# Attention with sinks and a window, then a gated feed-forward layer, on one core: batch 0 in runs of six column tiles, with the order of its requests and of the next batches' loads changed

## The chip, the cores and the metric

The kernel runs on one core of a Trainium2 chip. The metric is device time in microseconds, the median of several executions. Five engines work side by side, each through its own list of instructions in order: TensorE (PE: matrix products, with weight loads beside them), VectorE (DVE), ScalarE (ACT), GpSimd (POOL) and SyncE (SP, here only a queue that issues transfers). POOL also issues transfers, those that turn f32 into bf16 on the way.

## The reference

Inputs: q, k, v of 4 batches, 8 heads, 768 positions, 64 wide, in f32; the weights of the second layer, 512 x 1536 twice and 1536 x 512 once.

```python
scores = scale * np.matmul(q, k.transpose(0, 1, 3, 2))
is_sink = pos[None, :] < int(n_sink)              # n_sink = 4
rel = pos[:, None] - pos[None, :]
in_window = (rel >= 0) & (rel < int(window))      # window = 128
scores = np.where(is_sink | in_window, scores, -1000000000.0)
scores = scores - np.max(scores, axis=-1, keepdims=True)
a = np.exp(scores)
a = a / (np.sum(a, axis=-1, keepdims=True) + 1e-09)
attn_out = np.matmul(a, v)
...
x = attn_out.transpose(0, 2, 1, 3).reshape(B * S, H * D)      # 3072 x 512
gate = np.maximum(x @ w_gate, 0.0)
out = (gate * (x @ w_val)) @ w_out                            # 3072 x 512
```

## The kernel before

The work falls into 16 units: unit i is a pair of heads, number i % 4, of batch i // 4. A unit passes through these steps.

- Its k and q are loaded (`load_half` in two halves for batch 0, L110; `load_rows` for the others, L159) into one of three pairs of buffers, `kf` and `qf`, and turned to bf16 on POOL (`cast_half`, `cast_rows`) into one of two pairs, `kn` and `qn`.
- They are turned so that the 64 values of a head lie on partitions, into one of four `KQ` tiles: on PE for batches 0 and 1 (`T_half`, H in the plan, and `T`), and through DRAM with a transposing transfer for batches 2 and 3 (`to_dram` writes `kqd`, "td" in the plan; `turn` reads it back). POOL copies the keys of the odd tiles and the sinks (`odd_tiles`, L185).
- `Sg` (S in the plan, with unit and segment) makes a segment of scores on PE, ACT takes exp from PSUM into `ee` (L298), and DVE multiplies by the mask (L300).
- `W` makes the products with v on PE (L325) and divides on DVE (L330, L331) into `xn`. v comes through `load_v` and a cast (`cast_v`, L134).
- `X` turns `xn` on PE (L342) and ACT copies it to `xT` (L345). For batches 2 and 3 this goes through DRAM too (`x_to_dram`, `x_turn`).

`xT` of a batch, 512 x 768, is the input of the second layer. `chunk(b, g, m)` makes column tile m (128 of the 1536) of half g of the positions: four products with `wg` (L360), a Relu on ACT (L363, `gs`), four with `wv` (L365), and a product of both on DVE into `hT` (L367). Its two PSUM banks come from three, in turn. Half 0 of batch 0 has 372 positions and needs only the first three tiles of attention (part 0 of W and X), half 1 has 396. `ffn2` then multiplies `hT` by `wo` (L392).

Everything is in an order written out by hand. First comes a head: the loads and part 0 of batch 0's attention. Then 96 slots follow, each one chunk. In each slot the list `prep` is issued first (casts, loads, requests), then the chunk, then the list `plan` (H, T, S, W, X of a unit), then three `ffn2` products from slot 24 on. Batch 0's column tiles go in two runs, so that the first weights serve both halves before the later ones are needed:

```python
for b, runs in enumerate((((0, 8), (8, FM)),) + ((((0, FM),),) * (B - 1))):
    slots += [(b, g, m) for m0, m1 in runs for g in range(2) for m in range(m0, m1)]
```

So slots 0 to 7 are half 0 of tiles 0 to 7, slots 8 to 15 half 1 of the same, 16 to 23 tiles 8 to 11. The weights come in pieces, `load_w(m0, m1)`, issued by POOL between its casts: tiles 0-1, 2-3 and 4-5 in the head, 6-7 in slot 1 behind the first cast of later v tiles, 8-11 in slot 9, `wo` in slot 14.

Every engine and queue keeps to its list. A transfer on SP waits, in its place, for the buffer that it fills and for the eighth transfer before it. `gate(u)` (L138) is a memset of two elements of `kf` on DVE; the load of that buffer must wait for it, and so can't be issued before DVE has reached that place of its list. Before the change the loads of units 4 to 6 have such a gate in slot 6, and halves 4 and 5 one in the head (L423).

Of the kernel before, what the change touches and what calls it, by code (L numbers as in the profile page):

```python
# [21 lines left out]
def kernel(  # L22
# [12 lines left out]
    nc = tc.nc  # L35
# [80 lines left out]
    def cast_half(c, copies=(nc.gpsimd.tensor_copy, nc.gpsimd.tensor_copy)):  # L116
        for src, dst, copy in ((kf, kn, copies[0]), (qf, qn, copies[1])):
            copy(half(dst, c).rearrange("p (n h d) -> p h n d", n=3, h=2),
                                  half(src, c).rearrange("p (h n d) -> p h n d", n=3, h=2))
# [4 lines left out]
    def load_v(b, j, r0=0, r1=128):  # L124
        r1 = min(r1, S - VROW[j])

        parts = [(0, 4, 0), (4, 16, VROW[j] + 4), (16, 128, VROW[j] + 16)] if j in (1, 3, 5) else [(0, 128, VROW[j])]
        for a0, a1, s0 in parts:
            a1 = min(a1, r1)
            if r0 <= a0 < a1:  # L130
                nc.sync.dma_start(out=vf[a0:a1, j, :, :], in_=v[b, :, s0:s0 + a1 - a0, :].rearrange("h s d -> s h d"))
# [4 lines left out]
    def gate(u):  # L136

        nc.vector.memset(kf[u.i % NQ][0:1, 0:2], 0.0)  # L138
# [209 lines left out]

    gvn = [0]

    def chunk(b, g, m):
        assert all((b, p, g) in ready for p in range(NP)), (b, g)
        x, h = xT[b % 2], hT[b % 2]
        cut = CUT if b else CUT0
        c = slice(0, cut) if g == 0 else slice(cut, S)
        n = c.stop - c.start
        gp, vp = G[gvn[0] % 3], G[(gvn[0] + 1) % 3]
        gvn[0] += 2
        for ko in range(KO):
            nc.tensor.matmul(out=gp[:, 0:n], lhsT=wg[:, ko, m * 128:(m + 1) * 128], rhs=x[:, ko, c],  # L360
                             start=ko == 0, stop=ko == KO - 1)
        gs = gspool.tile([128, S - CUT0], F32, name="gs")
        nc.scalar.activation(gs[:, 0:n], gp[:, 0:n], Act.Relu, bias=0.0, scale=1.0)  # L363
        for ko in range(KO):
            nc.tensor.matmul(out=vp[:, 0:n], lhsT=wv[:, ko, m * 128:(m + 1) * 128], rhs=x[:, ko, c],  # L365
                             start=ko == 0, stop=ko == KO - 1)
        nc.vector.tensor_tensor(h[:, m, c], gs[:, 0:n], vp[:, 0:n], op=Alu.mult)  # L367

    OP = [[G[3][:]], [G[3][:], PP[0][:, 0, :], PP[1][:, 0, :]]]
# [29 lines left out]
    with tc.manual_schedule():  # L399
# [25 lines left out]
        for j in range(3):  # L425
            cast_v(0, j, copy=dve if j == 2 else nc.gpsimd.tensor_copy)
        load_w(2, 4)
        for c in range(4, 8):
            load_half(c)
            if c < 6:  # L430
                cast_half(c)
        for j in range(3, 7):
            load_v(0, j)
        load_w(4, 6)
        Sg(U[2], 0, PP[1])
        Sg(U[2], 3, PP[0])
        W(U[0], 0, g[2])
# [5 lines left out]
        X(U[1], 0, g[1])  # L443
        W(U[3], 0, PP[0][:, 0, :])
        X(U[2], 0, g[2])
        X(U[3], 0, g[3])
        setup2(1)
        setup2(2)


        slots = []

        for b, runs in enumerate((((0, 8), (8, FM)),) + ((((0, FM),),) * (B - 1))):
            slots += [(b, g, m) for m0, m1 in runs for g in range(2) for m in range(m0, m1)]
        plan = [[] for _ in slots]
        at = {}
# [3 lines left out]
            at[st] = s  # L460
            plan[s].append(st)

        for s, w in {0: "H0", 1: "S04 H1", 2: "S02 H2 S14", 3: "S12 H3", 4: "S24 S22", 5: "S34 S32", 6: "W01 W11",
                     7: "X01 W21 X11 W31 X21 X31"}.items():
            for y in w.split():
                put(s, y, 0)
        for s, w in {8: "T0", 9: "T1", 10: "S00 S01", 11: "T2", 12: "S02 S10", 13: "T3 S11", 14: "S12 S20", 15: "S21",
                     16: "S22 S30", 17: "S31 S32", 19: "W0", 20: "W1 X0", 21: "W2 X1", 22: "W3 X2", 23: "X3 F3"}.items():
            for y in w.split():
                if y[0] == "F":  # L470
                    plan[s].append(("F", int(y[1:]), 0))
                else:
                    put(s, y, 1)
        for b, sl in ((2, {28: "S00 S01", 30: "S02 S10", 32: "S11 S12", 34: "S20 S21", 35: "W0", 36: "S22 S30",
# [3 lines left out]
            for s, w in sl.items():  # L478
                for y in w.split():
                    put(s, y, b)  # L480
        prep = [[] for _ in slots]
        prep[1] += [("half", 6), ("half", 7), ("setup3",), ("v", 0, 3), ("w", 6, 8), ("v", 0, 4), ("v", 0, 5), ("v", 0, 6)]
        prep[6] += [("load", 4), ("load", 5), ("load", 6)]
        prep[8] += [("kq", 4), ("load", 7), ("lv", 1)]
        prep[9] += [("kq", 5), ("w", 8, 12)]
        prep[10] += [("kq", 6)]
        prep[11] += [("kq", 7)]
        prep[14] += [("v", 1, 0), ("v", 1, 1), ("v", 1, 2), ("v", 1, 3), ("wo",), ("v", 1, 4), ("v", 1, 5), ("v", 1, 6)]
        for i, ts in ((8, (18, 21, 22, 25)), (9, (19, 22, 23, 26)), (10, (21, 24, 25, 28)), (11, (23, 25, 27, 30)),
                      (12, (28, 31, 33, 36)), (13, (30, 33, 35, 38)), (14, (32, 35, 37, 42)), (15, (34, 37, 39, 43))):  # L490
            for t, what in zip(ts, ("rows", "castrows", "td", "turn")):
                prep[t].append((what, i))
            assert at["S", i - NP, 2] < ts[3] < at["S", i, 0] - 1, i
            prep[at["S", i, 0] - 1].append(("sinks", i))
            prep[at["W", i, 0] + 1].append(("xd", i))
            prep[at["W", i, 0] + 3].append(("xturn", i))

        for b, s0, s1 in ((2, 24, 28), (3, 44, 47)):
            for j in range(7):
                prep[s0 + j].append(("lv", b, j))  # L500
                prep[s1 + j].append(("v", b, j))

        f2 = deque()
        for s, (b, g, m) in enumerate(slots):
            for x in prep[s]:
                if x[0] == "kq":
                    cast_rows(U[x[1]])
                elif x[0] == "load":
                    if x[1] < 7:
                        gate(U[x[1]])  # L510
                    load_rows(U[x[1]])
                elif x[0] == "half":
                    cast_half(x[1])
                elif x[0] == "w":
                    load_w(*x[1:])
                elif x[0] == "wo":
                    for c in range(3):
                        load_wo(c)
                elif x[0] == "rows":
                    load_rows(U[x[1]])  # L520
                elif x[0] == "castrows":
                    cast_rows(U[x[1]])
                elif x[0] == "td":
                    to_dram(U[x[1]])
                elif x[0] == "setup3":
                    setup3()
                elif x[0] == "xd":
                    x_to_dram(U[x[1]])
                elif x[0] == "xturn":
                    x_turn(U[x[1]])  # L530
                elif x[0] == "turn":
                    turn(U[x[1]])
                elif x[0] == "sinks":
                    odd_tiles(U[x[1]], nc.gpsimd.tensor_copy)
                elif x[0] == "lv":
                    for j in x[2:] or range(7):
                        load_v(x[1], j)
                else:
                    cast_v(*x[1:])
            chunk(b, g, m)  # L540
            if s == 23:
                f2 += [lambda t=t, mm=mm: ffn2(0, t, mm) for t in range(6) for mm in range(FM)]
            for what, i, x in plan[s]:
                if what == "F":
                    for _ in range(i):
                        f2.popleft()()
                elif what == "X":
                    X(U[i], x if i < NP else None)
                elif what == "T":
                    T(U[i])  # L550
                elif what == "H":
                    T_half(NP + i, queries=nc.scalar.copy if i == 0 else nc.vector.tensor_copy)
                elif what == "S":
                    Sg(U[i], x)
                else:
                    W(U[i], x if i < NP else None)
            for _ in range(3 if s > 23 else 0):
                if f2:
                    f2.popleft()()
            if b > 0 and m == FM - 1:  # L560
                f2 += [lambda b=b, t=t, mm=mm: ffn2(b, t, mm) for t in range(3 * g, 3 * g + 3) for mm in range(FM)]
# [38 lines left out]
```

## Time and profile before

| what | value |
|---|---|
| median of 6 runs | 258.53 us (256.26 to 259.59) |
| profiled execution, its own time | 258.84 us |
| its span, first to last instruction | 256.9 us |
| TensorE clock granted | 1.0 throughout |
| PE busy | 239.5 us, 93% |
| DVE, ACT, POOL busy | 120.9, 120.0, 70.3 us |
| moved by transfers | 40.07 MB, mean 156 GB/s |

The times below are microseconds from the start of the span. A line of instructions reads: start, duration, engine, line, operation, output <- inputs, shape, and in brackets the idle time of the engine before it, with what ended it. A line of waits reads: engine and line <- what it waited for: total, times, longest.

### The profile page before, as it was taken

The page shows a single profiled execution, that of the slowest core. Times are in us where ns is not written, and L with a number is a line of the kernel's source. Part 1 is how long each engine was busy: PE and PEld are TensorE (multiplying, and loading weights), DVE is VectorE, ACT ScalarE, POOL GpSimd, SP SyncE. Part 2 cuts the span into 40 slices and gives each one's busy share as a digit, 9 for nine tenths or more (in the row PEclk, how much of TensorE's full clock was granted, in tenths as well). Part 3 has the DMA queues.
Part 4 walks back from the last instruction along what each step waited for, and adds up shares of the span by engine and source line. Part 5 has one row for each costly group of instructions (what it writes and reads, how often), then busy time and mean ns, then how long its engine had stood idle before and what let it go on. Part 6 is the DMA issues. An engine that isn't in the chain of part 4 may idle for free.

```text
span 256.9 us, 5323 instructions
## 1 busy us (share of the span) xinstructions
PE 239.5 (93%) x2084; PEld 139.6 (54%) x2084; DVE 120.9 (47%) x226; ACT 120.0 (47%) x219; POOL 70.3 (27%) x125
## 2 busy tenths in 40 slices
PE   7786958899699999999999999999999999999994
PEld 3353546465476555656655555666555555555443
DVE  5563865298975246665534555664322322322000
ACT  3855934789535367544325573623333233333211
POOL 7737832959723305641002700000000000000000
PEclk9999999999999999999999999999999999999999
DMA  6999699999999789999699601334210111110232
GB/s 204 189 251 244 115 197 337 192 211 301 243 267 268 186 223 273 349 277 213 161 182 236 141 3 53 87 84 128 81 41 3 41 41 43 43 41 0 84 120 84
DMA packets 75681, 40.07 MB, mean 156 GB/s; under 512 B 53512, under 2 KB 72712, under 8 KB 75656
## 3 DMA queue, kind: packets, MB, share of 16 engines
q1 hardware_dynamic: 67560, 34.10, 51.7%
q0 software_dynamic: 6864, 4.72, 12.6%
q10 hardware_dynamic: 1232, 0.92, 1.1%
q8 instruction: 16, 0.26, 0.4%
q14 instruction: 9, 0.07, 0.1%
HBM read 28.48 MB, written 11.25 MB: 155 GB/s over the span
## 4 chain that ended last, share of the span: by engine, by line
PE 74%; DMA 11%; ACT 4%; issue 4%; DVE 3%; POOL 2%; SPq 1%; POOLq 0%; ACTq 0%; DVEq 0%
PE g L365 20%; PE g L360 20%; PE g L392 20%; PE pp L325 5%; DMA kf<-in_k_dram 5%; DMA vf<-in_v_dram 4%; PE pp L392 3%; PE pp L290 3%; ACT ee L298 2%; DMA wv<-in_moe_w_val_dram 2%; DVE ee L300 1%; ACT ot L396 1%; DVE hT L367 1%; PE g L342 1%; SPq L113 1%
## 5 line engine op out<-in xcount | busy, mean ns | idle before, releaser
L367 DVE TENSOR_TENSOR hT<-gs,g 128x384 bf16<-128x384 f32 (+2 forms) x96 | 52.9, 552 | 91.9 <-PE g L365 86.9
L363 ACT ACTIVATE gs<-g 128x384 f32<-128x384 f32 (+2 forms) x96 | 47.7, 497 | 82.4 <-PE g L360 81.5
L360 PE MATMUL g<-xT,wg 128*128 128x384 bf16 (+2 forms) x384 | 78.5, 326 | 4.5 <-DVE hT L367 2.5
L365 PE MATMUL g<-xT,wv 128*128 128x384 bf16 (+2 forms) x384 | 78.1, 326 | 3.4 <-DMA wv<-in_moe_w_val_dram 3.3
L392 PE MATMUL g<-wo,hT 128*128 128x512 bf16 x240 | 64.0, 379 | 0.4 <-ACT ot L396 0.2
L360 PEld LDWEIGHTS <-wg 128*128 128x128 bf16 x384 | 36.1, 98 | 35.2 <-issue 2.7
L365 PEld LDWEIGHTS <-wv 128*128 128x128 bf16 x384 | 37.2, 98 | 29.8 <-DMA wv<-in_moe_w_val_dram 5.2
L298 ACT ACTIVATE ee<-pp 128x838 bf16<-128x838 f32 (+4 forms) x50 | 43.0, 904 | 10.5 <-PE pp L290 10.2
L300 DVE TENSOR_TENSOR ee<-ee,msk 128x838 bf16<-128x838 bf16 (+3 forms) x44 | 35.5, 815 | 14.2 <-ACT ee L298 13.6
L392 PEld LDWEIGHTS <-hT 128*128 128x128 bf16 x276 | 25.4, 98 | 24.2 <-issue 1.3
L134 POOL CAST vn<-vf 128x512 bf16<-128x512 f32 x27 | 17.9, 689 | 24.3 <-DMA vf<-in_v_dram 24.3
L325 PEld LDWEIGHTS <-ee 128*128 128x128 bf16 x512 | 17.9, 97 | 3.1 <-issue 1.2
L396 ACT COPY ot<-g 128x512 f32<-128x512 f32 x20 | 11.7, 587 | 16.1 <-PE g L392 15.3
L166 POOL CAST kn<-kf 128x768 bf16<-128x768 f32 x12 | 10.4, 867 | 28.1 <-DMA kf<-in_k_dram 13.4
L325 PE MATMUL pp<-vn,ee 128*128 128x65 bf16 x488 | 17.5, 193 | 0.0
L331 DVE TENSOR_TENSOR xn<-pp,rn 128x896 bf16<-128x896 f32 (+2 forms) x18 | 17.0, 943 | 0.6
L290 PEld LDWEIGHTS <-KQ 64*128 64x128 bf16 x328 | 11.0, 94 | 10.7 <-issue 9.1
L290 PE MATMUL pp<-KQ 64*128 64x3 bf16 (+5 forms) x316 | 15.8, 221 | 0.6 <-DVE KQ L259 0.6
L166 POOL CAST qn<-qf 128x768 bf16<-128x768 f32 x12 | 10.9, 906 | 1.0 <-DMA qf<-in_q_dram 0.9
L185 POOL COPY KQ<-KQ 128x372 bf16<-128x372 bf16 x12 | 6.9, 572 | 15.0 <-ACT KQ L258 8.7
L392 PE MATMUL pp<-wo,hT 128*128 128x512 bf16 x36 | 8.1, 379 | 0.0
L345 ACT COPY xT<-g 128x372 bf16<-128x372 bf16 (+2 forms) x10 | 5.4, 544 | 5.7 <-PE g L342 5.7
(80 smaller groups left out, 107.5 us busy)
## 6 DMA issues: line engine op xcount, KB each, us to landing
out_dram<-ot SPq DMA_DIRECT2D x23, 256.0 KB
kf<-in_k_dram SPq DMA_DIRECT2D x12, 384.0 KB
qf<-in_q_dram SPq DMA_DIRECT2D x12, 384.0 KB
vf<-in_v_dram SPq DMA_DIRECT2D x12, 256.0 KB
vf<-in_v_dram SPq DMA_DIRECT2D x12, 224.0 KB
kf<-in_k_dram SPq DMA_DIRECT2D x8, 192.0 KB
wo<-in_moe_w_out_dram POOLq DMA_DIRECT2D x3, 512.0 KB, 12.0
kqd<-qn SPq DMA_DIRECT2D x8, 192.0 KB
```

Of the source, the lines that this page charges most:

```text
L134: copy(vn[b % 2][0:rows, j, :, 0:64], vf[0:rows, j, :, :])
L166: nc.gpsimd.tensor_copy(dst[u.i % 2][:].rearrange("p (n h d) -> p h n d", n=NR, h=2), src[u.i % NQ][:].rearrange("p (h n d) -> p h n d", n ...
L290: nc.tensor.matmul(out=at[h][:, c0:c1], lhsT=kE[t][64 * h:64 * h + 64, x0:x0 + 128], rhs=qT[t][64 * h:64 * h + 64, q0:q0 + c1 - c0], start ...
L298: nc.scalar.activation(x, ps[:, :, b0:n], Act.Exp, bias=0.0, scale=scale)
L300: nc.vector.tensor_tensor(x, x, msk[:, g, b0:n].unsqueeze(1).to_broadcast([128, 2, n - b0]), op=Alu.mult)
L325: nc.tensor.matmul(out=at[h][:, c:c + 65], lhsT=ee[u.i % NE][:, g, h, c0:c0 + 128], rhs=vn[u.b % 2][:, j, 2 * u.p + h, 0:65], start=c == 0 ...
L331: nc.vector.tensor_tensor(x.rearrange("p t (h d) -> p h t d", h=2), o[:, :, :, 0:64], r.unsqueeze(3).to_broadcast([128, 2, n, 64]), op=Alu ...
L360: nc.tensor.matmul(out=gp[:, 0:n], lhsT=wg[:, ko, m * 128:(m + 1) * 128], rhs=x[:, ko, c], start=ko == 0, stop=ko == KO - 1)
L363: nc.scalar.activation(gs[:, 0:n], gp[:, 0:n], Act.Relu, bias=0.0, scale=1.0)
L365: nc.tensor.matmul(out=vp[:, 0:n], lhsT=wv[:, ko, m * 128:(m + 1) * 128], rhs=x[:, ko, c], start=ko == 0, stop=ko == KO - 1)
L367: nc.vector.tensor_tensor(h[:, m, c], gs[:, 0:n], vp[:, 0:n], op=Alu.mult)
L392: nc.tensor.matmul(out=op, lhsT=hT[b % 2][:, m, t * 128:(t + 1) * 128], rhs=wo[:, m, :], start=m == 0, stop=m == FM - 1)
```

## The change

Six things move; what is computed stays.

1. Batch 0's column tiles go in runs of six: slots 0 to 5 are half 0 of tiles 0 to 5, 6 to 11 half 1, 12 to 23 the same with tiles 6 to 11. The plan of batch 0 and batch 1 is fitted to it (W and X of batch 0's second part in slot 5, T0 in slot 6, the first S of batch 1 in slot 9).
2. In the head the loads of halves 6 and 7 and of v tiles 3 to 6 go behind a new memset on DVE, after `setup2`. The weights of tiles 4-5 are requested ahead of half 5's cast, and `setup3` is put ahead of the casts of halves 6 and 7.
3. The weights of tiles 6-7 are requested in slot 8 and those of tiles 8-11 in slot 10.
4. The loads of units 4 to 6 are in slot 4 and have no gate; the loads of units 8 and 9 (batch 2) in slots 18 and 19 have one.
5. Batch 2's casts, writes and turns, and its S and W, are a slot earlier for most units, its v too.
6. `chunk` takes a function `mid`: it makes the first two products with `wg` and the first two with `wv`, calls it, and then makes the rest. In slots 0 and 6 `mid` is the X of unit 3.

```diff
-    def chunk(b, g, m):
+    def chunk(b, g, m, mid=None):
...
+        def products(w, ps, kos):
+            for ko in kos:
+                nc.tensor.matmul(out=ps[:, 0:n], lhsT=w[:, ko, m * 128:(m + 1) * 128], rhs=x[:, ko, c],
+                                 start=ko == 0, stop=ko == KO - 1)
+        k0 = 2 if mid else 0
+        if mid:
+            products(wg, gp, range(k0))
+            products(wv, vp, range(k0))
+            mid()
+        products(wg, gp, range(k0, KO))
         gs = gspool.tile([128, S - CUT0], F32, name="gs")
         nc.scalar.activation(gs[:, 0:n], gp[:, 0:n], Act.Relu, bias=0.0, scale=1.0)
+        products(wv, vp, range(k0, KO))
         nc.vector.tensor_tensor(h[:, m, c], gs[:, 0:n], vp[:, 0:n], op=Alu.mult)
...
         load_w(2, 4)
-        for c in range(4, 8):
+        for c in (4, 5):
             load_half(c)
-            if c < 6:
-                cast_half(c)
-        for j in range(3, 7):
-            load_v(0, j)
+        cast_half(4)
         load_w(4, 6)
+        cast_half(5)
...
-        X(U[3], 0, g[3])
+        g0 = g[3]
         setup2(1)
         setup2(2)
+        nc.vector.memset(kf[0][0:1, 0:2], 0.0)
+        for c in (6, 7):
+            load_half(c)
+        for j in range(3, 7):
+            load_v(0, j)
...
-        for b, runs in enumerate((((0, 8), (8, FM)),) + ((((0, FM),),) * (B - 1))):
+        for b, runs in enumerate((((0, 6), (6, FM)),) + ((((0, FM),),) * (B - 1))):
...
-        for s, w in {0: "H0", 1: "S04 H1", 2: "S02 H2 S14", 3: "S12 H3", 4: "S24 S22", 5: "S34 S32", 6: "W01 W11",
-                     7: "X01 W21 X11 W31 X21 X31"}.items():
+        for s, w in {0: "H0", 1: "H1 S04", 2: "S02 H2 S14", 3: "S12 S24 H3", 4: "S22 S34 S32",
+                     5: "W01 W11 X01 W21 X11 W31 X21"}.items():
...
-        for s, w in {8: "T0", 9: "T1", 10: "S00 S01", 11: "T2", 12: "S02 S10", 13: "T3 S11", 14: "S12 S20", 15: "S21",
-                     16: "S22 S30", 17: "S31 S32", 19: "W0", 20: "W1 X0", 21: "W2 X1", 22: "W3 X2", 23: "X3 F3"}.items():
+        for s, w in {6: "T0", 8: "T1", 9: "S00 S01", 10: "T2", 11: "S02 S10", 12: "T3", 13: "S11 S12", 14: "S20",
+                     15: "S21 S22", 16: "S30", 17: "S31 S32", 19: "W0", 20: "W1 X0", 21: "W2 X1", 22: "W3 X2",
+                     23: "X3 F3"}.items():
...
-        for b, sl in ((2, {28: "S00 S01", 30: "S02 S10", 32: "S11 S12", 34: "S20 S21", 35: "W0", 36: "S22 S30",
-                           37: "W1", 38: "S31 S32", 40: "W2", 41: "W3"}),
+        for b, sl in ((2, {27: "S00 S01", 29: "S02 S10", 31: "S11 S12", 33: "S20 S21", 34: "W0", 35: "S22 S30",
+                           36: "W1", 37: "S31 S32", 38: "W2", 39: "W3"}),
...
-        prep[1] += [("half", 6), ("half", 7), ("setup3",), ("v", 0, 3), ("w", 6, 8), ("v", 0, 4), ("v", 0, 5), ("v", 0, 6)]
-        prep[6] += [("load", 4), ("load", 5), ("load", 6)]
-        prep[8] += [("kq", 4), ("load", 7), ("lv", 1)]
-        prep[9] += [("kq", 5), ("w", 8, 12)]
-        prep[10] += [("kq", 6)]
+        prep[1] += [("setup3",), ("half", 6), ("half", 7), ("v", 0, 3), ("v", 0, 4), ("v", 0, 5), ("v", 0, 6)]
+        prep[4] += [("load", 4), ("load", 5), ("load", 6)]
+        prep[6] += [("kq", 4), ("load", 7), ("lv", 1)]
+        prep[8] += [("kq", 5), ("w", 6, 8)]
+        prep[10] += [("kq", 6), ("w", 8, 12)]
...
-        for i, ts in ((8, (18, 21, 22, 25)), (9, (19, 22, 23, 26)), (10, (21, 24, 25, 28)), (11, (23, 25, 27, 30)),
+        for i, ts in ((8, (18, 20, 21, 24)), (9, (19, 21, 22, 25)), (10, (20, 23, 24, 27)), (11, (22, 24, 26, 29)),
...
-        for b, s0, s1 in ((2, 24, 28), (3, 44, 47)):
+        for b, s0, s1 in ((2, 23, 27), (3, 44, 47)):
...
+        mid = {0: lambda: X(U[3], 0, g0), 6: lambda: X(U[3], 1)}
...
                 elif x[0] == "load":
-                    if x[1] < 7:
-                        gate(U[x[1]])
                     load_rows(U[x[1]])
...
                 elif x[0] == "rows":
+                    if x[1] in (8, 9):
+                        gate(U[x[1]])
                     load_rows(U[x[1]])
...
-            chunk(b, g, m)
+            chunk(b, g, m, mid.pop(s, None))
```

The four numbers behind a unit of batch 2 or 3 are the slots in which its rows are loaded, cast, written to `kqd` and turned.

More of the change, by code (lines that the diff above doesn't have):

```diff
@@ L349 @@
     gvn = [0]
-    def chunk(b, g, m):
-        assert all((b, p, g) in ready for p in range(NP)), (b, g)
+    def chunk(b, g, m, mid=None):
         x, h = xT[b % 2], hT[b % 2]
@@ L358, in chunk @@
         gvn[0] += 2
-        for ko in range(KO):
-            nc.tensor.matmul(out=gp[:, 0:n], lhsT=wg[:, ko, m * 128:(m + 1) * 128], rhs=x[:, ko, c],
-                             start=ko == 0, stop=ko == KO - 1)
+        def products(w, ps, kos):
[7 more added lines that the diff above has]
+            mid()
+        assert all((b, p, g) in ready for p in range(NP)), (b, g)
+        products(wg, gp, range(k0, KO))
         gs = gspool.tile([128, S - CUT0], F32, name="gs")
         nc.scalar.activation(gs[:, 0:n], gp[:, 0:n], Act.Relu, bias=0.0, scale=1.0)
-        for ko in range(KO):
-            nc.tensor.matmul(out=vp[:, 0:n], lhsT=wv[:, ko, m * 128:(m + 1) * 128], rhs=x[:, ko, c],
-                             start=ko == 0, stop=ko == KO - 1)
+        products(wv, vp, range(k0, KO))
         nc.vector.tensor_tensor(h[:, m, c], gs[:, 0:n], vp[:, 0:n], op=Alu.mult)
```

## Prediction, made before the changed kernel ran

> **What bounds the kernel now.** I read the two summary parts first, then a table by stretches of the span, then what TensorE (PE) waited for, and last the instructions around each of its pauses.
>
> ```profile
> PE 239.5 (93%) x2084; PEld 139.6 (54%) x2084; DVE 120.9 (47%) x226; ACT 120.0 (47%) x219; POOL 70.3 (27%) x125
> PE   7786958899699999999999999999999999999994
> DMA  6999699999999789999699601334210111110232
> ```
>
> PE is the bound; its idle time, 256.9 - 239.5 = 17.4 us, stands almost wholly in the first eleven of forty slices. There the transfers (DMA row) are busy too.
>
> ```profile
> 22.00:34.00 12.00, 8.54 (x95) 4.79 (x94) 8.34 (x15) 9.30 (x21) 9.17 (x19) 1.00 0.97 162
> 34.00:46.00 12.00, 9.83 (x140) 7.06 (x140) 6.01 (x16) 4.85 (x10) 2.11 (x4) 1.00 0.96 289
> 46.00:60.00 14.00, 12.50 (x129) 7.72 (x128) 8.89 (x13) 11.29 (x18) 10.79 (x19) 1.00 1.13 196
> 60.00:72.00 12.00, 9.55 (x109) 5.92 (x108) 11.39 (x14) 7.31 (x13) 9.04 (x12) 1.00 1.11 280
> 72.00:140.00 68.00, 67.84 (x655) 41.02 (x654) 35.01 (x57) 32.23 (x53) 18.75 (x30) 1.00 1.01 238
> 140.00:257.00 117.00, 113.28 (x791) 63.54 (x788) 39.31 (x68) 41.89 (x76) 5.78 (x12) 1.00 0.22 65
> ```
>
> Columns: stretch, length, busy PE, weight loads, DVE, ACT, POOL, clock, DMA share, GB/s. From 22 to 72 PE idles 9.6 us, from 72 to 140 only 0.2, and the 3.7 at the end are the tail that the change doesn't touch. So what it can win lies before 72 us, and what PE wins there it keeps, provided that batch 2 and 3 data are still in time.
>
> ```profile
> PE g L365 <- DMA wv<-in_moe_w_val_dram: 3.3, 3, 2.0
> PE g L360 <- DVE hT L367: 2.5, 1, 2.5
> PE g L360 <- DMA wg<-in_moe_w_gate_dram: 1.7, 1, 1.7
> PE g L254 <- POOL kn L166: 0.7, 1, 0.7
> PE g L342 <- DVE xn L331: 0.6, 2, 0.4
> PE g L342 <- ACT xT L345: 0.6, 1, 0.6
> ```
>
> Weights cost 5.0 us: wv of tiles 0-1 0.36 (till 18.81), of tiles 2-3 1.96 (till 24.89), and wg and wv of tiles 6-7 1.73 and 1.00 (till 36.26). The last pair has a cause on POOL:
>
> ```profile
> 29.43 0.61 POOL L134 CAST vn<-vf 128x512 bf16<-128x512 f32 x1 [0.94 <-DMA vf<-in_v_dram]
> 29.98 0.74 POOL L190 DMA_DIRECT2D wg<-in_moe_w_gate_dram  x1
> 30.71 0.75 POOL L190 DMA_DIRECT2D wv<-in_moe_w_val_dram  x1
> ```
>
> The request for tiles 6-7 stands behind a cast that waits for v; from 28 to 32 us the transfers are nearly idle.
>
> The 2.45 us behind DVE have another cause:
>
> ```profile
> 64.97 3.40 DVE L300 TENSOR_TENSOR ee<-ee,msk 128x998 bf16<-128x998 bf16 x1
> 68.29 0.53 DVE L367 TENSOR_TENSOR hT<-gs,g 128x372 bf16<-128x372 f32 x1
> 65.47 0.82 POOL L166 CAST kn<-kf 128x768 bf16<-128x768 f32 x1
> ```
>
> That mask product takes 0.99 in the mean; here it takes 3.40, while POOL runs the four row casts of units 8 and 9 back to back (65.47 to 69.0). The hT product behind it frees the bank for which PE waits.
>
> **The change, part by part.** No arithmetic is added: the order of instructions has as many PE, DVE, ACT and POOL entries as before. So PE's 239.5 stay, and only waits change. A slot is one chunk; a chunk is 8 products of 0.16 us, 1.3 us.
>
> *Slot 0 (X of unit 3 inside).* PE now does X2, two wg and two wv products, X3, then the other four. In the trace wv of tiles 0-1 lands at 18.8, and until 17.5 the same transfers compete (halves 4, 5), so I leave it at 18.6. Before, X3 ran at 17.24, while wv was awaited; now it stands behind the wait: 18.6 + 0.33 + 0.35 + copy (L345, 0.5) gives xT at 19.8, the last three products end at about 20.4 against 19.55. Minus 0.85 us. Bounds: +0.6 if wv is there at 17.3 (0.35 of xn wait and X3's copy covered), -1.0.
>
> *Requests of halves 6, 7 and v tiles 3-6 later.* They now wait for a DVE memset at the end of setup2 (about 18.6) instead of going out from 13.05. Ten microseconds of weights gain: the POOL queue moved about 65 KB/us (as bf16) beside them and 130 alone (12 to 14 us), so wv of tiles 2-3 lands at about 21.5 instead of 24.84, before the slot 2 product wants it (23.6 after the loss above). Plus 1.96; lower bound 0.5, if the queue is no faster. Halves 6 and 7 were late anyway (casts at 21.5 to 25.7); issued at 18.7 with no queue ahead they land at about 23.3 and 25, and setup3's memsets (2.9 us on POOL), now ahead of their casts, run from 19 to 22 in that gap. PE wants them at 24.3 and 26.8: nothing. If the cover goes (half 5's cast late by a microsecond), 0.7.
>
> *Six column tiles per run.* Tiles 6-7 are wanted only in slot 12, so the 1.73 + 1.00 go: plus 2.73. What is late next: S04 to S32 now lie in slots 1 to 4 instead of 1 to 5. From S04's exp to gs of slot 5 ACT has eight exps of 0.85 us (L298), four gs of 0.5 and two key copies of 0.8: 10.4 us. PE has four chunks, eight S of 0.33 and two T of 0.5: 8.8. ACT so sets the pace, 1.6 over, and hT, rn and xn in a row on DVE (0.55 + 0.21 + 0.69) before X01 add some 0.3. I charge 1.9 (bounds 0.8 and 2.7; v tiles 3-6, cast by 31.5 to 32.5 as against 33.9, fall inside). X of unit 3 inside slot 6 hides the 0.58 wait on xT's copy: plus 0.58.
>
> *Batch 1 rows without a gate.* Units 4-6 go out behind v at about 28 instead of 34.9. T0 is a whole slot away from T1 now, so most of T1's 0.68 + 0.26 goes: plus 0.6 (bounds 0 and 1.5 with the 0.56 on L259).
>
> *Weights for tiles 6-7 and 8-11 after casts of units 5 and 6.* POOL reaches them at about 42 and 46; before, tiles 8-11 went at 47.7 and landed at 54.3 and 58.6, the second 10.2 after its issue, beside the v of batch 1. They are wanted two slots earlier, wv at about 53.8. With v of batch 1 mostly through by 46, 7 to 8 us are likelier than 10.2: minus 0.5 (bounds 0 and 3.2).
>
> *Gate for units 8, 9.* Their rows wait for DVE's memset at slots 18, 19 (about 63 on the new scale), behind the last mask products; so the four casts come at about 67, when DVE has W's products from PSUM. Plus 2.2 of 2.45 (seven v casts of 0.61 still lie beside mask products; bounds 0 and 2.45). Queued behind the waiting request on SP are the loads of units 9, 10 and the writes to kqd; PE wants unit 8 at slot 27.
>
> [...]
>
> Sum: -0.85 + 1.96 + 2.73 - 1.9 + 0.58 + 0.6 - 0.5 + 2.2 = 4.8. The profiled execution took 258.84 (span 256.9, 1.9 around it); minus 4.8 is 254.0. The median of the six runs is 0.3 lower: 253.7.
>
> **Rivals.** *A: batch 2 comes late (slower).* From the gate at 63: 0.5 + loading 4.4 (unit 10: issued 70.31, cast at 74.97), then 17.1 from first cast to odd tiles as unit 8 took (65.47 to 82.59) + 0.7 = 85.7; wanted at 81.56 + 4 slots of 1.95 - 4.8 = 84.6. With the gate a microsecond later S00 waits 2.1. Worse, units 10 and 11 followed unit 8 by 17.9 and 25.3, and S20 and S30 come only 13.9 and 19.4 after S00: another 4.0 and 1.9 would follow, 8.0 in all: 253.7 + 8.0 = 261.7. It decides once the gate opens after about 62. Against it: wo (1.5 MB) is then through early, where the 17.1 were spent beside it, and unit 10's lag in the trace is in part SP's wait for an output tile (88.2), which moves with PE. *B: the weights' wait only turns into ACT's and v's.* Then the head wins nothing (-0.85 + 1.96 + 2.73 - 1.9 + 0.58 = 2.5 lost): 256.2. For it: ACT is busy 9.3 of 12 us from 22 to 34 already. Against: v lands no later than before. *C: weights late in slot 14* by the full 3.2: 253.7 + 2.7 = 256.4. For it the 10.2 us; against it the idle queue.
>
> **How the numbers follow.** Forecast 0.70 (own range 250.2 to 256), A 0.11, B 0.10, C 0.09. The range is 250.2 (ACT charge 0.8, slot 0 free, T waits gone) to 258.0, which takes in B, C and both together in part, and leaves A out. A measurement of this kernel can tell about 1% from nothing: faster, below 255.9, is 0.68 of the forecast's 0.70 and half of B and C near the limit, 0.05: 0.73; slower is A, 0.11; the rest 0.16.
>
> **What would show it.** Right: no PE wait on wv in slot 2 or on weights before slot 12; PE begins slot 7 some 2.5 us early by the work done; mask products of slots 14 to 17 all under 1.3 us and no pause at slot 19; unit 8's odd tiles done before S00. Wrong: PE waiting on KQ in slots 27 to 35 (A), on ACT through slots 3 to 6 by over 3 us (B), on wv at slot 14 by over 2 us (C).

## The result, and the profile after

The changed kernel is a little slower: median 260.12 us over 28 executions (257.02 to 267.62) against 257.77 over 63 of the kernel before (255.36 to 262.62). The ratio is 1.0085, interval 1.0065 to 1.0104. The forecast was 253.7 with a range up to 258.0, so both miss. The ratios leave out the executions more than 1.5% above the fastest of their kernel (9 of these 28; 6 of 12 in e3 and in e7), so the table of the experiments gives the medians over all executions beside them.

The profiled execution after took 258.06 us, 2 us under its median: one of its best. The one before took 258.84, above its median. So these two must not be subtracted from one another to explain the medians; they serve to find the places. First the two lines of the summary and the table by stretches, with the columns of the one before:

```profile
PE 239.5 (94%) x2084; PEld 140.3 (55%) x2084; DVE 116.7 (46%) x226; ACT 120.3 (47%) x219; POOL 69.1 (27%) x125
PE   7978879979999996799999999999999999999994
```

```profile
22.00:34.00 12.00, 9.34 (x121) 5.89 (x119) 8.47 (x16) 9.42 (x21) 7.18 (x14) 1.00 1.06 242
34.00:46.00 12.00, 11.09 (x147) 7.74 (x144) 5.76 (x12) 7.42 (x13) 6.08 (x12) 1.00 1.11 281
46.00:60.00 14.00, 12.45 (x125) 7.53 (x124) 10.29 (x16) 10.90 (x17) 11.58 (x19) 1.00 1.01 155
60.00:72.00 12.00, 12.00 (x175) 8.41 (x174) 9.51 (x19) 6.74 (x12) 2.56 (x4) 1.00 1.09 261
72.00:140.00 68.00, 63.93 (x570) 37.71 (x568) 32.75 (x52) 31.47 (x51) 20.45 (x33) 1.00 1.00 240
```

PE's work is the same 239.5 us. From 22 to 72 us it idles 5.1 us instead of 9.6; between 60 and 72 the pause behind the mask product is gone altogether. But from 72 to 140, where it idled 0.2, it now idles 4.1: the 6 and 7 that stand sixteenth and seventeenth in the PE row. The list of what PE waited for says with what:

```profile
PE pp L325 <- POOL vn L134: 2.5, 3, 1.6
PE pp L290 <- POOL KQ L181: 2.5, 1, 2.5
PE g L362 <- DMA wv<-in_moe_w_val_dram: 2.5, 2, 1.4
```

The weights cost 2.5 us instead of 5.0 (1.07 in slot 0, 1.40 in slot 14). New are KQ of unit 10, awaited by its first scores S20 (2.49, till 100.45), and v for W0 of batch 2 (1.58, till 105.04). S00, the first scores of batch 2, starts at 84.03, behind the chunk of slot 27; before, a slot later in the plan, at 90.74. Of these 6.7 us one slot is 1.95 and an earlier head in this execution 0.7. So the changes up to there won 4.1 us, near the forecast's 4.8, and batch 2 took them back. How it did is in two lists. SP's, before and after:

```profile
84.71 0.58 SPq L131 DMA_DIRECT2D vf<-in_v_dram  x1
88.21 0.36 SPq L397 DMA_DIRECT2D out_dram<-ot  x1
...
90.86 2.54 SPq L175 DMA_TRANSPOSE KQ<-kqd  x1
```

```profile
84.46 0.58 SPq L131 DMA_DIRECT2D vf<-in_v_dram  x1
85.14 0.52 SPq L171 DMA_DIRECT2D kqd<-qn  x1
85.71 1.65 SPq L171 DMA_DIRECT2D kqd<-kn  x1
87.40 1.12 SPq L131 DMA_DIRECT2D vf<-in_v_dram  x3
88.62 0.50 SPq L405 DMA_DIRECT2D out_dram<-ot  x1
89.22 2.04 SPq L175 DMA_TRANSPOSE KQ<-kqd  x1
```

Before, SP has time to spare: it stands 2.9 us waiting for an output tile, and issues the turn of unit 10 (the last line) at 90.86, together with S00. After, its list runs with no gap over 0.2 us from 75 us on, as the gate let the loads of units 8 and 9 out at 64.94 instead of 57.86; the turn of unit 10 goes out at 89.22, now 5.2 us after S00. Behind it on SP stand the rows of unit 12, and POOL's list waits for them ahead of unit 10's odd tiles:

```profile
96.96 0.83 POOL L166 CAST kn<-kf 128x768 bf16<-128x768 f32 x1 [4.96 <-DMA kf<-in_k_dram]
98.44 0.83 POOL L166 CAST qn<-qf 128x768 bf16<-128x768 f32 x1 [0.65 <-DMA qf<-in_q_dram]
99.21 0.61 POOL L134 CAST vn<-vf 128x512 bf16<-128x512 f32 x1
99.77 0.50 POOL L185 COPY KQ<-KQ 128x372 bf16<-128x372 bf16 x1
```

POOL sits idle for 5 us in front of a cast for batch 3, and the copy for which PE stands (the last line) still comes three instructions later. Before, POOL waited for the same cast, and longer, but PE came for the copy only at 104.64; the last line here is PE after:

```profile
97.34 0.83 POOL L166 CAST kn<-kf 128x768 bf16<-128x768 f32 x1 [8.52 <-DMA kf<-in_k_dram]
100.45 0.49 POOL L185 COPY KQ<-KQ 128x372 bf16<-128x372 bf16 x1
104.64 0.63 PE L290 MATMUL pp<-KQ 64*128 64x244 bf16 x12
```

```profile
100.45 0.53 PE L290 MATMUL pp<-KQ 64*128 64x252 bf16 x10 [2.49 <-POOL KQ L181]
```

PE now comes for it 7 us earlier (97.69), and the copy 0.7 us earlier (99.77).

### The profile page after: what moved, and what is told of

It is laid out like the page before. It is cut to its first block, busy times and chain, and to the rows that moved or that the text cites. A ratio compares the mean times of both kernels' runs of the same rounds, so it can differ in the third digit from the quotient of the medians.

```text
span 256.1 us, 5323 instructions
## 1 busy us (share of the span) xinstructions
PE 239.5 (94%) x2084; PEld 140.3 (55%) x2084; DVE 116.7 (46%) x226; ACT 120.3 (47%) x219; POOL 69.1 (27%) x125
## 3 DMA queue, kind: packets, MB, share of 16 engines
q0 software_dynamic: 6864, 4.72, 12.6%
## 4 chain that ended last, share of the span: by engine, by line
PE 74%; DMA 13%; SPq 5%; POOL 3%; issue 2%; ACT 1%; DVE 1%; POOLq 0%; DVEq 0%; ACTq 0%
PE g L362 40%; PE g L400 20%; PE pp L325 4%; DMA vf<-in_v_dram 4%; DMA qf<-in_q_dram 4%; SPq L131 4%; DMA wv<-in_moe_w_val_dram 3%; PE pp L290 3%; PE pp L400 3%; DMA kf<-in_k_dram 1%; PE g L267 1%; POOL vn L134 1%; POOL qn L166 1%; SPq L113 1%; PE pp L394 1%
## 5 line engine op out<-in xcount | busy, mean ns | idle before, releaser
L300 DVE TENSOR_TENSOR ee<-ee,msk 128x838 bf16<-128x838 bf16 (+3 forms) x44 | 31.7, 728 | 17.6 <-ACT ee L298 16.6
L134 POOL CAST vn<-vf 128x512 bf16<-128x512 f32 x27 | 18.8, 716 | 29.1 <-DMA vf<-in_v_dram 29.1
L166 POOL CAST qn<-qf 128x768 bf16<-128x768 f32 x12 | 10.3, 857 | 2.2 <-DMA qf<-in_q_dram 2.2
```

Of the source, the lines that this page charges most:

```text
L134: copy(vn[b % 2][0:rows, j, :, 0:64], vf[0:rows, j, :, :])
L166: nc.gpsimd.tensor_copy(dst[u.i % 2][:].rearrange("p (n h d) -> p h n d", n=NR, h=2), src[u.i % NQ][:].rearrange("p (h n d) -> p h n d", n ...
L300: nc.vector.tensor_tensor(x, x, msk[:, g, b0:n].unsqueeze(1).to_broadcast([128, 2, n - b0]), op=Alu.mult)
```

## The experiments

Ratios are to the kernel before, run on the same chip. Edits are shown against the changed kernel unless said otherwise. "Medians" are over all executions, the run's and those of the kernel before beside it. The last column is read from the run's profile: the time from the start of S00 to POOL's copy of unit 10's odd tiles. S20, which needs that copy, comes 13.7 to 13.9 us after S00 where nothing holds PE.

| run | gate 8, 9 | batch 2 | halves 6, 7 | weights 6-11 | ratio | medians | copy after S00 |
|---|---|---|---|---|---|---|---|
| changed kernel | yes | slot earlier | late | late | 1.0085 [1.0065, 1.0104] | 260.12, 257.77 | 15.7 |
| e3 | yes | old slots | late | late | 1.0001 [0.9960, 1.0042] | 258.89, 257.46 | 12.4 |
| e4 | no | slot earlier | late | late | 1.0223 [1.0180, 1.0265] | 262.85, 257.46 | 9.5 |
| e5 | yes | slot earlier | early | late | 1.0112 [1.0071, 1.0154] | 260.30, 257.49 | 15.9 |
| e7 | yes | old slots | early | late | 0.9982 [0.9943, 1.0022] | 258.85, 257.49 | 12.0 |
| e8 | yes | old slots | early | early | 0.9966 [0.9934, 0.9999] | 256.14, 257.49 | 14.1 |
| e12 | yes | slot earlier | early | early | 1.0053 [1.0011, 1.0094] | 258.58, 258.17 | 16.0 |
| e11 | no | slot earlier | early | early | 0.9956 [0.9915, 0.9996] | 257.12, 257.94 | 9.5 |
| e10 | no | old slots | early | early | 0.9844 [0.9786, 0.9903] | 254.66, 257.94 | 9.7 |
| e6: kernel before, with the gate | yes | old slots | as before | as before | 1.0156 [1.0107, 1.0206] | 261.34, 257.49 | 15.8 |
| kernel before (its profile; e9) | no | old slots | as before | as before | 1 | | 9.7; 10.4 |

**The changed kernel again** (e1, no edit), to see what its usual execution looks like.

> The changed kernel once more, beside the others on one chip. Three theories for its time. P (POOL's list): PE arrives at batch 2 some 4 to 5 us earlier, but the odd-tile copies of unit 10 and the last v casts stand on POOL behind the casts of units 12 and 13, which wait for their rows; PE stalls before S of unit 10 and in W of unit 8, together 3 to 5 us. G (gate): the rows of units 8 and 9 come so late that the whole chain of batch 2 is late, stalls from unit 8's first S on. C (clock): the granted TensorE clock is lower than for the kernel before. All expect a ratio of 1.005 to 1.012 here; P and G expect the stalls in this profile too, C a clock below that of the kernel before by 0.5% or more.

Measured: median 261.75, ratio 1.0153 [1.0099, 1.0207], above what all three theories gave; the profiled one had a span of 260.6 and a mean clock of 0.987. Both waits of batch 2 are there again, 1.15 and 2.47. A third is new: PE's line of the first product of slot 2's H, then three stretches of 2 us, then the cast on POOL that it waited for.

```profile
25.21 0.34 PE L267 MATMUL g<-ident,kn 128*128 128x128 bf16 x3 [2.94 <-POOL kn L118]
```

```profile
24.00:26.00 2.00, 0.56 (x6) 0.34 (x6) 0.00 (x0) 0.00 (x0) 1.01 (x2) 1.00 1.36 214
26.00:28.00 2.00, 2.00 (x15) 0.96 (x13) 0.85 (x2) 1.56 (x5) 1.26 (x3) 0.53 0.89 172
28.00:30.00 2.00, 2.00 (x23) 1.08 (x22) 0.81 (x2) 0.81 (x2) 1.34 (x2) 0.61 0.92 246
```

```profile
24.65 0.50 POOL L118 CAST kn<-kf 128x384 bf16<-128x384 f32 x1 [2.21 <-DMA kf<-in_k_dram]
```

Half 6 was requested at 18.81 and its cast could begin at 24.65. From 20 to 22 us, beside the weights, the transfers moved 207 GB/s in all; in e3 and e4, with pauses of 2.52 and 2.85 at this place, 203 and 191; in e2, where it is 0.97, 234, and in the profile after, with 0.61, 274. That the late request stood behind the weights is an estimate from these rates, not shown. The third number from the right is the granted clock: after the pause it is 0.53 and 0.61 for two stretches, which loses 2 x 0.47 + 2 x 0.39 = 1.7 us more. The same came after the 2.47 us pause at 107.87 (0.51 and 0.63 from 108 to 112). Neither of the two profiled executions compared above had such a stretch.

**The gate on the kernel before** (e6): that kernel, and only the gate added.

```diff
                 elif x[0] == "rows":
+                    if x[1] in (8, 9):
+                        gate(U[x[1]])
                     load_rows(U[x[1]])
```

> The kernel before with one part of the change alone: the gate on the loads of units 8 and 9 in slots 18 and 19. The term of 2.2 us stands if the pause of 2.45 us at slot 19 goes and nothing takes its place: ratio 0.988 to 0.994. If the later rows make batch 2 late (unit 10's odd tiles were 3.5 us ahead of their use, unit 11's 2.5), stalls of 1 to 4 us come before S of units 10 and 11, or in W: ratio 0.995 to 1.01.

Measured: 1.0156, worse than both ranges given; 261.04 us on average against 257.06, so the gate alone costs 4.0 us. The stretch of the old pause, and PE's waits in batch 2:

```profile
60.00:72.00 12.00, 11.96 (x179) 8.44 (x178) 10.02 (x19) 7.07 (x12) 4.09 (x6) 1.00 1.02 204
```

```profile
102.95 0.53 PE L290 MATMUL pp<-KQ 64*128 64x252 bf16 x10 [1.52 <-POOL KQ L181]
...
107.82 0.22 PE L325 MATMUL pp<-vn,ee 128*128 128x65 bf16 x2 [1.93 <-POOL vn L134]
```

The pause at slot 19 goes (11.96 busy of 12, as forecast), and the two waits of the changed kernel appear in a kernel that has nothing else of the change. That is the gate's doing, shown by itself. In the profile PE waits 4.5 us in all for KQ and v between 91 and 109 us, 2.1 more than the pause of 2.45 that goes, and the granted clock, 0.96 in the mean of 100 to 140 us, adds an estimated 0.04 x 40 = 1.6: near the 4.0.

**No gate in the changed kernel** (e4): the two lines above taken out.

> The gate on units 8 and 9 left out, all else as changed. Their rows come some 15 us earlier. G: the stalls of batch 2 go, ratio 0.985 to 0.995, less what the collision of casts and mask products costs. P: the casts of units 12 and 13 still wait for rows that SP issues behind the turn of unit 10, so most of the stall stays; and POOL's casts of units 8 and 9 lie again beside mask products in slots 15 to 18, at 0 to 2.5 us: ratio 1.0 to 1.02.

Measured: 1.0223, the slowest of all and beyond both ranges given. Batch 2's waits are gone (PE busy 68.00 of 68 us from 72 to 140), but:

```profile
58.03 1.42 PE L362 MATMUL g<-xT,wg 128*128 128x372 bf16 x4 [2.99 <-DMA wg<-in_moe_w_gate_dram]
62.96 1.42 PE L362 MATMUL g<-xT,wv 128*128 128x372 bf16 x4 [3.51 <-DMA wv<-in_moe_w_val_dram]
```

Four products take 1.42 instead of 0.80: the granted clock is 0.50 from 58 to 68 us. The rows of units 8 and 9, issued by 51.24 (in the profile after from 64.94 on), now travel beside the weights of tiles 8 to 11, which this change requests a slot later and needs two slots earlier: from 46 to 60 us the transfers move 255 GB/s, in the profile after 155, and PE's first products with that `wv` start at 62.96, in the profile after at 56.00. So in the changed kernel the gate also guards the late weights; taking it out alone shows nothing good.

**Batch 2 back at its old slots** (e3), gate kept:

```diff
-        for b, sl in ((2, {27: "S00 S01", 29: "S02 S10", 31: "S11 S12", ...
+        for b, sl in ((2, {28: "S00 S01", 30: "S02 S10", 32: "S11 S12", ...
-        for i, ts in ((8, (18, 20, 21, 24)), (9, (19, 21, 22, 25)), (10, (20, 23, 24, 27)), (11, (22, 24, 26, 29)),
+        for i, ts in ((8, (18, 21, 22, 25)), (9, (19, 22, 23, 26)), (10, (21, 24, 25, 28)), (11, (23, 25, 27, 30)),
-        for b, s0, s1 in ((2, 23, 27), (3, 44, 47)):
+        for b, s0, s1 in ((2, 24, 28), (3, 44, 47)):
```

> Batch 2's loads, casts, writes, turns, S, W and v at the slots that they had before the change; the gate on units 8 and 9 and all else of the change stay. P: S of unit 10 comes a slot (1.95 us) later and W of unit 8 too, with POOL's casts of units 12 and 13 where they were: the two stalls shrink by 2 to 3 us in all, ratio 0.992 to 1.0. G: the rows of units 9 to 11 are a slot later as well, stalls stay about as they are, ratio 1.005 to 1.015.

Measured: 1.0001, no difference from before (by the medians half a percent slower). KQ is awaited no more; v still is (1.51 and 0.34 at 105). So asking for batch 2 a slot earlier costs something of its own, in a kernel whose SP list can't follow: 0.8% against the changed kernel's ratio, 1.5% against e1, which ran beside it.

**The casts of batch 3 later** (e2): units 12 to 15 cast in slots 34 to 40 instead of 31 to 37, so that unit 10's odd tiles don't stand behind them.

```diff
-                      (12, (28, 31, 33, 36)), (13, (30, 33, 35, 38)), (14, (32, 35, 37, 42)), (15, (34, 37, 39, 43))):
+                      (12, (28, 34, 36, 39)), (13, (30, 36, 38, 41)), (14, (32, 38, 40, 42)), (15, (34, 40, 42, 44))):
```

> The casts of units 12 to 15 two to three slots later (12: slot 34, 13: 36, 14: 38, 15: 40; writes and turns behind them), so that unit 10's and 11's odd tiles and the v casts of batch 2 stand ahead of them on POOL. P: both stalls (2.5 and 1.6 us) go, the ratio falls to 0.985 to 0.995. G: the stalls stay, as rows of units 8 and 9 are as late, ratio as in the repeat. C: clock and time as in the repeat or a little worse.

Measured: 1.0152 [1.0090, 1.0215], as e1; the gain that P expected did not come. Batch 2 has its data (PE busy 40.00 of 40 us from 100 to 140, one wait of 0.49 ahead of it), so it was indeed the order on POOL for which PE stood. But batch 3 is late now:

```profile
145.26 0.28 PE L290 MATMUL pp<-KQ 64*128 64x252 bf16 x4 [2.54 <-POOL KQ L181]
```

and in this execution the weights of slots 12 to 14 cost 3.5 us. The wait was moved, not removed.

**Halves 6 and 7 early again** (e5): behind halves 4 and 5, without the memset.

```diff
-        for c in (4, 5):
+        for c in (4, 5, 6, 7):
             load_half(c)
...
-        nc.vector.memset(kf[0][0:1, 0:2], 0.0)
-        for c in (6, 7):
-            load_half(c)
```

> The changed kernel without the memset in the head: halves 6 and 7 are requested right behind halves 4 and 5, v tiles 3 to 6 behind them. Theory H (head): in the usual execution of the changed kernel PE waits 2.5 to 2.9 us in slot 2 for the cast of half 6, whose request starts at 18.8 beside the weights, and the pause is followed by some 3.4 us at a granted clock of 0.5, which costs another 1.7. H expects the wait in slot 2 to be under 1 us, the clock to stay 1.0 in 22 to 34, and 2 to 4 us less than the changed kernel: ratio 0.998 to 1.007. Rival W: the weights of tiles 2-3 then come later by as much, PE waits 1.5 to 2 us for them in slot 2 as in the kernel before, and nothing is won: ratio 1.008 to 1.015.

Measured: 1.0112. The wait on half 6 is gone, and the one on wv is back:

```profile
23.10 0.80 PE L362 MATMUL g<-xT,wv 128*128 128x372 bf16 x4 [1.82 <-DMA wv<-in_moe_w_val_dram]
```

Weights and halves travel together before 25 us (in the profile of the kernel before 0.38 MB by POOL's queue and 0.57 by SP's from 18 to 22), and here the weights are late by about as much as the half was. It isn't always so: of the runs below, with the halves as early, e7, e8 and e12 wait 1.1 to 1.7 us for this wv, e10 and e11 don't.

**Combinations.** e7 is e3 and e5 together. e8 is e7 with the weights of tiles 6 to 11 requested in slot 6, behind unit 4's cast, and with unit 13's cast two slots later. e10 is e8 without the gate. e11 and e12 take the changed kernel's own batch 2, with the halves and weights early, without and with the gate.

```diff
-        prep[6] += [("kq", 4), ("load", 7), ("lv", 1)]
-        prep[8] += [("kq", 5), ("w", 6, 8)]
-        prep[10] += [("kq", 6), ("w", 8, 12)]
+        prep[6] += [("kq", 4), ("w", 6, 8), ("w", 8, 12), ("load", 7), ("lv", 1)]
+        prep[8] += [("kq", 5)]
+        prep[10] += [("kq", 6)]
```

Expected of e7:

> Batch 2 at its old slots (as in the third run) and the memset in the head gone (as in the fifth). If H and P are both right and add up, the pause in slot 2 and its slow clock go from a kernel that stood at 1.000: ratio 0.985 to 0.993, and the granted clock is 0.995 or more in the mean of the runs. If W, it stays at 0.997 to 1.003.

Expected of e8:

> As the run before it, and in addition the weights of tiles 6-7 and 8-11 requested in slot 6 behind unit 4's cast (some 35 instead of 43 and 46.5) and unit 13's cast two slots later (35), behind the last v cast of batch 2. The waits for weights at slots 12 and 14 (1.4 to 2.2 us) go, and of the wait in W of unit 8 (1.5 to 1.9) most: 2 to 3.5 us less than the run before it, ratio 0.975 to 0.985. Rival: the weights take the transfers from unit 7's rows and batch 1's v, and PE or POOL waits for these instead: no gain over the run before it.

Expected of e10:

> The eighth run's kernel (halves 6 and 7 early, weights of tiles 6 to 11 in slot 6, batch 2 at its old slots, unit 13's cast later) without the gate on units 8 and 9. Theory B (balance): the gate pays only where the weights come late, since it keeps these rows off the transfers; with the weights in slot 6 it only makes batch 2 late. Then the waits before S of unit 10, in W of unit 8 and for xT at slot 48 (3.4 us in all) go: ratio 0.982 to 0.992. Rival D: casts of units 8 and 9 lie beside the mask products again and PE pauses 1.5 to 2.5 us at slots 18 to 20: ratio 0.993 to 1.0.

Expected of e11:

> The changed kernel with three things undone or moved: no gate on units 8 and 9, halves 6 and 7 early, weights of tiles 6 to 11 in slot 6; batch 2 stays a slot early as in the change. B: no wait for weights after slot 5 (6.5 us in the run without the gate), batch 2's waits under 1 us: ratio 0.982 to 0.995, 6 to 10 us less than the run without the gate alone. If the early slots of batch 2 are the trouble in themselves, 1.5 to 3 us of waits before S of unit 10 and in W of unit 8 stay and the ratio is 0.997 to 1.007.

Expected of e12:

> The changed kernel with its gate for units 8 and 9 kept, but with halves 6 and 7 requested behind halves 4 and 5, and the weights of tiles 6 to 11 requested in slot 6. It differs from the run without the gate (0.9956) by the gate alone. Theory (the gate's pause is paid back by batch 2): no pause in slots 18 to 20 behind a mask product, but TensorE waits 3 to 4 us in all for KQ and vn between 88 and 110 us; the ratio to the kernel before is 1.000 to 1.008, that is about 2 us above the run without the gate. Rival (the gate costs nothing once the weights come early, since then nothing of batch 1 stands in its way): no pause in slots 18 to 20 and under 1 us of waits for KQ and vn; the ratio is 0.985 to 0.990. Either way no wait on weights of tiles 6 to 11 and no wait on half 6; the wait on wv of tiles 2 and 3 may return with up to 2 us.

Measured: 0.9982, 0.9966, 0.9844, 0.9956 and 1.0053 in this order. e7 stays where rival W put it, e8 gains less than expected, e11 lies at the edge of its first range, e10 and e12 inside one of theirs. With the weights requested in slot 6 no product waits for them in slots 12 to 14, in any of the four profiles (e7, where they are still late, waits 0.78 and 1.01). Once that is so, the gate can be judged in the changed kernel too: e12 over e11 is 1.0053 against 0.9956 (on two chips), e8 over e10 0.9966 against 0.9844, about 1% of loss by the gate in both (0.5 and 0.75% by the medians). e8 and e10 differ by the gate alone, and in their profiles PE reaches S00 at nearly the same time; first e8, then e10:

```profile
85.46 0.63 PE L290 MATMUL pp<-KQ 64*128 64x244 bf16 x12
99.53 0.49 POOL L185 COPY KQ<-KQ 128x372 bf16<-128x372 bf16 x1
```

```profile
85.61 0.63 PE L290 MATMUL pp<-KQ 64*128 64x244 bf16 x12
95.26 0.50 POOL L185 COPY KQ<-KQ 128x372 bf16<-128x372 bf16 x1
```

The copy of unit 10's odd tiles comes 4.3 us later with the gate. The PE waits of e12, with the gate, and then the DVE and PE lines of e11, without:

```profile
98.08 0.53 PE L290 MATMUL pp<-KQ 64*128 64x252 bf16 x10 [1.13 <-POOL KQ L181]
103.37 0.70 PE L325 MATMUL pp<-vn,ee 128*128 128x65 bf16 x18 [2.28 <-POOL vn L134]
```

```profile
60.34 4.73 DVE L300 TENSOR_TENSOR ee<-ee,msk 128x1014 bf16<-128x1014 bf16 x2 [0.45 <-ACT ee L298]
...
65.57 0.83 PE L362 MATMUL g<-xT,wg 128*128 128x396 bf16 x4 [2.51 <-DVE hT L375]
```

Without the gate the old collision of mask products and row casts returns, 2.51 here and 1.73 in e10; with it, the waits for KQ and v come to more in e12 (3.4, or 4.3 with the two short ones ahead); in e8 they are 0.57 and 0.94, and 1.87 for `xT` at slot 48 comes to them. e10 is faster than the kernel before: 0.9844, and 0.987 by the medians, from six executions. Its profiled execution took 253.60, span 251.8, clock 1.0; PE's waits over 0.5 us in it, from 14 us on, are 0.94 in slot 2, 0.61 and 0.85 behind KQ and v at 29 and 33, and the 1.73. Why e11 is slower than e10, with the same list up to slot 19, is open: its profile has pauses of 2.12 and 2.51 with half the clock behind each (0.50 from 22 to 24 us, 0.57 from 66 to 68), the first far ahead of the slots in which the two differ.

**The kernel before, once more** (e9), to see whether the forecast's base was typical.

> The kernel before once more, to see whether the pauses on which the prediction was built stand in another execution. If they are the kernel's own: a wait of 1.5 to 2.5 us for wv in slot 2, 2.3 to 3 us for the weights of tiles 6-7, and 2 to 2.8 us behind DVE at slot 19. If the pause at slot 19 belongs to the one execution (its own time of 258.84 lies 2 us above the mean of the runs at full clock), it is under 1 us here.

Measured: 257.51, span 255.6, clock 0.993. The pauses that answer to the three largest of the prediction:

```profile
23.64 0.80 PE L365 MATMUL g<-xT,wv 128*128 128x372 bf16 x4 [2.07 <-DMA wv<-in_moe_w_val_dram]
33.39 0.80 PE L360 MATMUL g<-xT,wg 128*128 128x372 bf16 x4 [0.56 <-DMA wg<-in_moe_w_gate_dram]
...
67.36 0.79 PE L360 MATMUL g<-xT,wg 128*128 128x372 bf16 x4 [2.48 <-DVE hT L367]
```

wv in slot 2 and the collision are as in the first profile (1.96 and 2.45). The wait for tiles 6-7 is not: 0.56 for wg, and 0.51 more behind ACT, where the first profile had 1.73 and 1.00 for the weights.

## Why the prediction was wrong, by its steps

**The step that failed: the gate on units 8 and 9, put at +2.2.** By itself it measured about -4.0 (e6), and it costs some 1% where the weights come early (e8 against e10, e12 against e11). The pause it removes was real and did go: no pause at slot 19 and mask products of at most 1.05 us in slots 14 to 17, as foretold. What was put at nothing is the delay of batch 2 by SP's own list: from the rows of unit 8 to the turn of unit 10 its instructions alone take 19 to 20 us (57.86 to 90.86 before, with 14 of gaps; 64.94 to 89.22 after, with 4). The last column of the table shows what the gate does: without it unit 10's copy comes 9.5 to 10.4 us after S00 in all five profiles, with it 12.0 to 16.0 in all nine (e1 15.4, e2 12.6), and S20 comes 13.7 to 13.9 after S00. e2 shows the other half of the path: the copy is late because on POOL it stands behind casts whose rows SP issues later still.

Rival A described this, units 10 and 11 included, and gave the point from which it decides as "about 62" beside a gate that the forecast itself put at "about 63" and that opened at 64.8. By its own sum S00 already waited 1.1 us at 63, and 1.7 if S00's own line is taken (90.74 - 1.95 - 4.8 = 84.0 in place of 84.6). It was priced at 8.0 us and held for 0.11; it came to 4.1 in the profile, though not in its parts: 2.49 for unit 10, and 1.58 for v, which it doesn't name, while units 8 and 11 were in time. Its price also counts unit 11's lag of 25.3 to the end of the copies and unit 10's 17.9 to their start; from start to start the first is 23.8, and the price 6.5. The number that should have moved the chance stood in the prediction's own text: by its estimate the gate opened late.

The gate was put in for the row of the 3.40 us mask product; what late rows cost stood only in rival A. e6, and e8, e10, e11 and e12 with the weights early, decide against the gate: the collision costs 1.7 to 2.5 us (1.73 in e10, 2.51 in e11), the late list more (waits of 3.4 in e8 and in e12, 4.5 in e6). e4 is the limit of that: with the weights as late as in the changed kernel, the early rows travel beside them, PE waits 6.5 us for the weights, and the kernel without the gate is the slower one (1.0223, e1 beside it 1.0153).

**Halves 6 and 7 late, costed at nothing.** In e1 half 6, requested at 18.81, landed at 24.6, not 23.3: the transfers were not free then (DMA share 1.41 from 20 to 22 us); and because wv came in time, PE reached the half earlier. The wait was 0.61 in the profile after and 0.97 in e2, but 2.94, 2.52 and 2.85 in e1, e3 and e4: in three of five profiles all of the +1.96 that the same step had won, and more. e5 is the other side of it. The rate of "130 alone (12 to 14 us)", from which the +1.96 was taken, was not alone: SP's queue moved 190 KB in these 2 us beside the 260 of POOL's.

**Not in the sum at all: the clock.** Of the 29 pauses of 1.5 to 3 us between 14 and 250 us in the fourteen profiles (e4's pair left aside) 11 were followed by about 3.4 us at half the clock, 1.7 us more each. In the executions compared the granted clock averages 0.990 after, and 0.995 in the 67 of the kernel before that stand beside the experiments; of the 2.1 us between their means (259.41 and 257.36) that is an estimated (0.9953 - 0.9902) x 257 = 1.3.

**The base.** The +2.73 for tiles 6-7 was read from one execution that had waited unusually long there; in e9 it would have been 0.56 to 1.07. The wait in slot 6 did go in every version with runs of six; where the weights are requested late, up to 0.83 of it (e2) came back at slot 12. Nor were the transfers "nearly idle" from 28 to 32 us: their share there is 0.38 and 0.30.

**What held.** Slot 0: forecast -0.85, in the profile 1.07 + 0.40 of waits in place of 0.70, so -0.77. ACT's pace and what comes with it: -1.9, measured 0.76 + 0.63 + 0.34 + 0.43 = 2.2; the size is right, but these waits end with DVE's copy of keys, v and `xn`, and only 0.21 more with ACT, so that ACT set the pace is not shown. T0 and T1: their waits are gone, and that on L259 too, +1.5, the upper bound. X in slot 6: only 0.17, as 0.41 of 0.58 stays. Weights in slot 14: -0.5 with bounds to 3.2; 1.40, and 2.23 over the two pieces in e1, 0.98 in e3, 2.70 in e2: mis-sized, inside its bounds; rival C's direction. In the profile at hand all of it up to slot 27 makes -0.77 + 1.35 (slot 2's 1.96 less 0.61) + 2.73 - 2.2 + 0.17 + 1.5 - 1.4 + 2.45 = 3.8, against the 4.1 read from S00: the sum came near for what it covered, in part by luck, as the 2.73 was unusual.

## What to carry to other kernels

Here the gate delayed not one transfer but every request behind it on SP's queue: the rows of unit 8 went out at 64.94 instead of 57.86, and the turn of unit 10, far behind them on that list, 5.2 us after S00 instead of together with it. So add up the queue's own issue time from the gate to the last request whose data PE will want, and compare it with the time that PE takes to get there, before crediting what the gate removes. The 4.1 us won upstream here were lost again in a queue downstream whose list had no gaps left to give (14 us of them before, 4 after); look for those gaps as one looks for idle time of an engine. And take what a wait is worth from more than one execution: here one step was three times smaller in the next profile.

## What the runs showed of the hardware that was not expected

- *Half the clock followed pauses of 1.57 us and more, but not all of them.* It came, for some 3.4 us each, after pauses of 2.94 and 2.47 (e1), 2.52 (e3), 2.51 and 2.12 (e11), 2.28 (e12), 2.07 (e9), 1.93 (e6), 1.87 (e8), 1.71 (e7) and 1.57 (e2); in the stretch of 12 us from 22 on the mean clock is 0.86 in e1, e3, e7, e9 and e11, 1.7 us lost. It did not follow eighteen others, among them 2.85 (e4, slot 2), 2.62 (e5), 2.49 (the profile after), 2.48 (e9, slot 19) and 1.73 (e10). So length alone doesn't decide; what does is open.
- *Two long waits near one another:* in e4 waits of 2.99 and 3.51, five microseconds apart, stood with a granted clock of 0.50 for 10 us, from 58 to 68.
- *A request on SP beside the weights took longer to land than forecast:* the 192 KB of keys of half 6 took 5.8 us in e1 (18.81 to 24.65) and in e3 (18.15 to 23.91), against the forecast's 4.6. In the profile after, requested at 17.89, they were there by 23.49, 5.6 at most; there SP's queue moved 360 KB and the weights' 190 from 20 to 22, 274 GB/s in all, where e1 and e3 moved 207 and 203. What decides the rate is open.
